# Key products as crossed 48x64 tiles, issued by turns with the corrected queries' products

## The chip, the cores and the metric

One core of one Trainium2 chip. The time is device microseconds (us) of one execution. A profile of one execution is taken apart from the timed runs. The engines go by short names: PE is TensorE (its matmuls; its weight loads stand apart as PEld), DVE is VectorE, ACT is ScalarE, POOL is GpSimd, SP is SyncE, which issues the loads.

## The reference

Three layers, one after the other: a delta-rule attention over 768 positions in 4 batches with 8 heads of 48, a mixing layer (Fourier transforms, then two products with a width of 1,536), and a gated layer with a product over positions. The change concerns the first:

```python
k_n = k / (np.linalg.norm(k, axis=-1, keepdims=True) + 1e-06)
state = np.zeros((B, H, D, D), dtype=np.float32)
for t in range(S):
    kt, vt, bt = (k_n[:, :, t], v[:, :, t], beta[:, :, t, None])
    y[:, :, t] = np.einsum('bhd,bhde->bhe', q[:, :, t], state)
    v_old = np.einsum('bhde,bhd->bhe', state, kt)
    state = state + bt[:, :, :, None] * np.einsum('bhd,bhe->bhde', kt, vt - v_old)
```

## The kernel before

**Tiling.** The positions are cut into chunks of 64; 4 batches of 12 chunks make 48 chunks, `bc`, in one order of their own (`SEQ`) in which the batches overlap. Heads go in four pairs, `hp`; of a pair one head lies on partitions 0 to 47 (or 63), the other on 64 to 111 (or 127). All products here are float32; one matmul of the program shows as two weight loads and two matmul records.

**Stages of a chunk.**
- `stage_a` (line 212): the key products. For each head pair, keys times queries and keys (64 rows by 128 columns) into the PSUM tile `pa` (bank X), which ACT copies out in two pieces (`copy_g`, lines 195 and 196) and, for later chunks, DVE masks (line 682).
- The triangular system made from them is solved on DVE in blocks of 8 chunks (`solve`, line 268): a generator, dealt out in shares to the steps (`part`, lines 615 and 616), so that DVE has solver work between the instructions that a step needs. `merge` and `diag` (lines 438 and 432) make the inverse of each chunk whole.
- `stage_b` (line 474): the inverse times keys and values, matmuls at line 480, copied out by ACT at line 482 (`WU`).
- `stage_c` (line 485): the products that correct the queries, 8 matmuls of 64 by 64 at line 495 into bank Y; DVE subtracts them at line 496 (`cw`).
- `stage_d` (line 499): state and output, 32 matmuls at lines 514 and 515.

**Forms of the key products.** Chunks 0 to 7 come first, by a path of their own (`pairs0`). Up to chunk 23 (`HEAD` is 24, line 31) `stage_a` does a pair of heads as two matmuls of 48 by 64, both on the diagonal of PE's array (`ROWS`, line 179; line 220): partitions 0 to 47 into output rows 0 to 63, partitions 64 to 111 into output rows 64 to 127. From chunk 24 on it does the pair as one matmul of 112 by 128 (line 222), for which the keys are laid out on the host as a block-diagonal matrix with zeros in the other blocks.

**Loads.** `load_kq` (line 202), on SP, in a pool of 5 buffers of 448 KB. For the head one load brings two chunks (`kc`: queries and keys only); from chunk 24 on one load brings one chunk (`kq`: queries, keys, and the block-diagonal keys twice as wide). The first five single loads stand in a table by step (`lead`, line 608); later ones are issued by `stage_a` of five chunks earlier. SP also issues the loads of the queries (`qt`), and of keys and values (`kv`), in program order.

**Steps.** The loop at line 609 runs `t` from -3 to 47. A step issues `stage_d(t)`, at times a `merge`, `stage_c(t + 1)`, a share of the solver, `stage_a` of a chunk 20 to 22 ahead (steps -3 to 1 for the rest of the head, steps 4 to 27 for chunks 24 to 47), `stage_b(t + 2)`, another `merge` at odd steps, and the rest of the solver's share. At the end of a step `self.chain()` fixes the order on each engine as written. Where `stage_c`'s chunk is the first of its batch, it has no products.

After the steps the mixing and gated layers follow (lines 693 to 1171).

Of the kernel before, what the change touches and what calls it, by code (L numbers as in the profile page):

```python
# [7 lines left out]
F32 = mybir.dt.float32  # L8
# [12 lines left out]
C = 64  # L21
# [45 lines left out]
class Kernel:  # L67
# [51 lines left out]
    def attention(self, cp, pg, pe, p, x, filler, after_solves):  # L119
# [59 lines left out]
        ROWS = (slice(0, D), slice(0, C)), (slice(64, 64 + D), slice(64, 64 + C))  # L179
# [22 lines left out]
        def load_kq(bc):  # L202
            if bc < HEAD:
                if 8 <= bc and bc % 2 == 0:
                    t = pe.tile([112, HP, 4 * C], F32, name="kq", bufs=CF["kq"]).rearrange("p a n -> p (a n)")
                    kqs[bc], kqs[bc + 1] = (t[:, i * HP * 2 * C : (i + 1) * HP * 2 * C].rearrange("p (a n) -> p a n", a=HP) for i in range(2))
                    load(out=t.rearrange("p (c n) -> p c n", c=2), in_=a["kc"][:, bc - 8 : bc - 6])
            elif bc < NBC:
                kqs[bc] = pe.tile([112, HP, 4 * C], F32, name="kq", bufs=CF["kq"])
                load(out=kqs[bc], in_=a["kq"][bc])  # L210

        def stage_a(bc):
            kq = kqs.pop(bc)
            if bc % 4 == 0:
                ring(bc)
            pa = self.bank("pa", [128, HP, 2 * C])
            for hp in range(HP):
                if bc < HEAD:
                    for r, q in ROWS:
                        nc.tensor.matmul(pa[q, hp], lhsT=kq[r, hp, C:], rhs=kq[r, hp], start=True, stop=True)  # L220
                else:
                    nc.tensor.matmul(pa[:, hp], lhsT=kq[:, hp, 2 * C :], rhs=kq[:, hp, : 2 * C], start=True, stop=True)
            if bc < HEAD:

                copy_g(gas[bc][:, :, C : 2 * C], pa[:, :, C:])
                nc.scalar.copy(out=gas[bc][:, :, :C], in_=pa[:, :, :C])
            else:
                copy_g(gas[bc][:, :, C : 2 * C], pa[:, :, C:])
                late.append((gas[bc][:, :, :C], pa[:, :, :C], mask_a(bc, C).to_broadcast([128, HP, C])))
            if bc < HEAD:  # L230
                if bc % 2 and bc + 2 * CF["kq"] < HEAD:
                    load_kq(bc + 2 * CF["kq"] - 1)
            else:
                load_kq(bc + CF["kq"])
            seen_a[0] = bc + 1
# [249 lines left out]
        def stage_c(bc):  # L485
# [6 lines left out]
            for hp in range(HP):  # L492
                for h in hs:

                    nc.tensor.matmul(pc[h, hp], lhsT=w[h, hp, :C], rhs=gas[bc][h, hp, : C + D], start=True, stop=True)  # L495
            nc.vector.tensor_sub(cw, qt, pc[:112])  # L496
# [111 lines left out]
        lead = {-2: (HEAD,), -1: (HEAD + 1,), 0: (HEAD + 2,), 1: (HEAD + 3,), 2: (HEAD + 4,)}  # L608
        for t in range(T0, NBC):
# [27 lines left out]
            if 0 <= t + 1 < NBC:  # L637
                stage_c(t + 1)
# [3 lines left out]
            if t + R + 2 < HEAD or HEAD <= t + R < NBC:  # L642
                stage_a(t + R + 2 * (t < 4))
            for bc in lead.get(t, ()):
                load_kq(bc)
# [690 lines left out]
def layout(q, k, v, beta, moe_w_ch1, moe_w_ch2, moe2_w_in, moe2_w_spatial, moe2_b_spatial, moe2_w_out):  # L1336
# [13 lines left out]
    kq = np.zeros((B, NC, 2, 64, HP, 4, C), f)  # L1350
    kq[:, :, :, :D, :, 0] = qt
    kq[:, :, :, :D, :, 1] = kt
    for h in range(2):
        kq[:, :, h, :D, :, 2 + h] = kt[:, :, h]
    kq = kq.reshape(NBC, 128, HP, 4 * C)[perm, :112]
    o["kq"] = kq

    o["kc"] = kq[8:HEAD, :, :, : 2 * C].transpose(1, 0, 2, 3).reshape(112, HEAD - 8, -1)
    o["kq0"] = np.stack([kq[:8, :, :, C : 2 * C], kq[:8, :, :, :C]]).transpose(0, 2, 1, 3, 4)
# [85 lines left out]
```

## Time and profile before

| what | us |
|---|---|
| timed runs, median | 853.3 |
| timed runs, lowest and highest | 852.4 and 856.03 |
| the profiled execution: span, first to last instruction | 849.6 |
| the profiled execution: its own time | not given beside the span |
| PE busy in the span | 806.9 |
| DVE busy | 606.6 |
| ACT busy | 419.8 |

The busy times of a page are sums over stages that differ. A stretch of the program is read from views that are cut to it: the busy time of each engine between two points of time, the timeline of an engine, and the list of who waited for whom. A wait that is marked "issue" is one for nothing that the profile shows. PEclk is the granted clock of PE as a share of full speed; the DMA share is the mean busy share of the 16 DMA engines.

### The profile page before, as it was taken

The page shows a single profiled execution, that of the slowest core. Times are in us where ns is not written, and L with a number is a line of the kernel's source. Part 1 is how long each engine was busy: PE and PEld are TensorE (multiplying, and loading weights), DVE is VectorE, ACT ScalarE, POOL GpSimd, SP SyncE. Part 2 cuts the span into 40 slices and gives each one's busy share as a digit, 9 for nine tenths or more (in the row PEclk, how much of TensorE's full clock was granted, in tenths as well). Part 3 has the DMA queues.
Part 4 walks back from the last instruction along what each step waited for, and adds up shares of the span by engine and source line. Part 5 has one row for each costly group of instructions (what it writes and reads, how often), then busy time and mean ns, then how long its engine had stood idle before and what let it go on. Part 6 is the DMA issues. An engine that isn't in the chain of part 4 may idle for free.

```text
span 849.6 us, 25166 instructions
## 1 busy us (share of the span) xinstructions
PE 806.9 (95%) x10507; PEld 769.6 (91%) x10507; DVE 606.6 (71%) x1791; ACT 419.8 (49%) x1070; POOL 6.3 (1%) x40
## 2 busy tenths in 40 slices
PE   7889999997888999999999999999999999999998
PEld 7778888876787999899999999999999899899998
DVE  7978898998969996692844992435678377586563
ACT  3669888887565544232233451223372462543632
POOL 1000000000000000000000000000000000000000
PEclk9779999999999999999999999999999999999999
DMA  8447666656532500001022410112001101101001
GB/s 241 109 124 181 187 170 191 166 162 177 148 106 60 204 1 1 1 1 29 1 72 80 131 34 22 38 57 66 29 3 47 64 12 46 57 23 59 32 1 56
DMA packets 57955, 67.63 MB, mean 80 GB/s; under 512 B 31857, under 2 KB 48978, under 8 KB 57842
## 3 DMA queue, kind: packets, MB, share of 16 engines
q1 hardware_dynamic: 57698, 65.89, 26.8%
q8 instruction: 82, 1.34, 0.7%
q14 instruction: 31, 0.25, 0.1%
q10 hardware_dynamic: 144, 0.15, 0.1%
HBM read 53.62 MB, written 4.72 MB: 69 GB/s over the span
## 4 chain that ended last, share of the span: by engine, by line
PE 67%; DVE 4%; issue 1%; ACT 1%; ACTq 0%
PE bankX L926 17%; PE bankY L939 15%; PE bankX L1124 10%; PE bankX L1104 6%; PE bankX L1072 6%; PE bankY L1152 5%; PE bankV L939 2%; PE bankX L739 2%; PE bankZ L1152 1%; PE bankX L755 1%; PE bankY L495 0%; PE bankX L733 0%; DVE cw L496 0%; DVE cvd L812 0%; PE bankY L515 0%
## 5 line engine op out<-in xcount | busy, mean ns | idle before, releaser
L939 PE MATMUL bankY<-w,hx 128*128 128x384 f32 x756 | 147.2, 336 | 0.0
L926 PE MATMUL bankX<-uh,w 128*128 128x384 f32 x504 | 137.7, 340 | 0.7 <-DVE ul L848 0.7
L939 PEld LDWEIGHTS bankY<-w,hx 128*128 128x128 f32 x756 | 132.4, 188 | 0.5 <-issue 0.3
L931 DVE SCALAR_TENSOR_TENSOR hx<-bankX,hx 128x384 fp32r<-128x384 f32 x84 | 46.2, 551 | 75.7 <-ACT hx L930 73.2
L930 ACT ACTIVATE hx<-bankX 128x384 fp32r<-128x384 f32 x84 | 41.2, 491 | 111.1 <-PE bankX L926 106.7
L926 PEld LDWEIGHTS bankX<-uh,w 128*128 128x128 f32 x504 | 92.1, 188 | 1.2 <-DVE ul L848 0.9
L1124 PE MATMUL bankX<-w,A 128*128 128x384 f32 x504 | 88.8, 334 | 0.0
L1124 PEld LDWEIGHTS bankX<-w,A 128*128 128x128 f32 x504 | 87.6, 188 | 0.0
L926 PE MATMUL bankX<-ul,w 128*128 128x384 f32 x252 | 85.1, 338 | 0.0
L495 PE MATMUL bankY<-gak,WU 64*64 64x112 f32 x704 | 45.3, 264 | 10.0 <-issue 6.2
L515 PE MATMUL bankY<-WU,gak 64*64 64x48 f32 x768 | 50.1, 224 | 1.1 <-ACT x L532 1.1
L1104 PE MATMUL bankX<-xh,s 128*128 128x384 f32 x192 | 50.0, 338 | 0.0
L314 DVE TENSOR_TENSOR Ts<-Ts,tm 128x108 f32<-128x108 f32 (+10 forms) x216 | 49.3, 265 | 0.9
L309 DVE TENSOR_TENSOR tm<-Ts 128x108 f32<-128x108 f32 (+10 forms) x216 | 48.9, 264 | 0.4
L1113 ACT CAST u<-hx 128x384 fp32r<-128x384 f32 x32 | 15.8, 513 | 66.0 <-DVE hx L1111 66.0
L514 PE MATMUL bankY<-WU,gak 64*64 64x48 f32 x704 | 43.8, 222 | 4.0 <-issue 4.0
L926 PEld LDWEIGHTS bankX<-ul,w 128*128 128x128 f32 x252 | 47.3, 188 | 0.0
L495 PEld LDWEIGHTS bankY<-gak,WU 64*64 64x64 f32 x704 | 35.6, 135 | 12.6 <-issue 7.1
L515 PE MATMUL bankY<-Sb,cw 48*64 48x48 f32 x704 | 46.0, 222 | 0.2
L514 PE MATMUL bankY<-Sb,cw 48*48 48x48 f32 x640 | 38.4, 208 | 8.2 <-DVE cw L496 4.9
L1072 PE MATMUL bankX<-s,xh 128*128 128x512 f32 x144 | 45.9, 395 | 0.0
L480 PE MATMUL bankY<-gak,TT 64*64 64x96 f32 x768 | 44.5, 256 | 1.2 <-ACT x L532 0.7
(237 smaller groups left out, 1827.7 us busy)
## 6 DMA issues: line engine op xcount, KB each, us to landing
kq<-in_kq_dram SPq DMA_DIRECT2D x24, 448.0 KB, 4.8
qt<-in_qt_dram SPq DMA_DIRECT2D x48, 196.0 KB, 4.1
gak<-in_kv_dram SPq DMA_DIRECT2D x48, 192.0 KB, 4.1
w<-in_w_dram SPq DMA_DIRECT2D x24, 384.0 KB, 6.9
out_dram<-x SPq DMA_DIRECT2D x24, 192.0 KB, 1.9
kq<-in_kc_dram SPq DMA_DIRECT2D x8, 448.0 KB, 9.8
x<-x SPq DMA_DIRECT2D x96, 36.0 KB, 1.9
s<-in_wi_dram SPq DMA_DIRECT2D x6, 512.0 KB, 4.3
```

The costliest lines, as they stand in the source:

```text
L309: nc.vector.tensor_tensor(out=tm, in0=T[:, r, k : k + 1].to_broadcast(sh), in1=T[:, k : k + 1, :k].to_broadcast(sh), op=MUL)
L314: nc.vector.tensor_add(o, o, tm)
L495: nc.tensor.matmul(pc[h, hp], lhsT=w[h, hp, :C], rhs=gas[bc][h, hp, : C + D], start=True, stop=True)
L514: nc.tensor.matmul(ps[C * i : C * i + n - C, hp], lhsT=k[:, C:n], rhs=u, start=not last, stop=end)
L515: nc.tensor.matmul(po[hs[1 - i], hp], lhsT=k[:, :C], rhs=u, start=not last, stop=end)
L926: nc.tensor.matmul(ph, lhsT=w1[f][i][:, c * 128 : c * 128 + 128], rhs=cur[k][:, c], start=(c + j == 0), stop=(c == 2 and j == 2))
L931: nc.vector.scalar_tensor_tensor(out=hl, in0=ph, scalar=0.0, in1=hh.bitcast(F32), op0=MAX, op1=SUB)
L939: nc.tensor.matmul(acc[t], lhsT=hx[i][:, t * 128 : t * 128 + 128], rhs=w2[e][k], start=(e == 0 and j == 0), stop=(e == 11 and j == 2),)
L1072: nc.tensor.matmul(pv, lhsT=xT[t][i][:, c, kk * 128 : kk * 128 + 128], rhs=wi[2 * c + 1][k], start=(c + j == 0), stop=(c == 2 and j == 2))
L1104: nc.tensor.matmul(pu, lhsT=wi[2 * c][i][:, f * 128 : f * 128 + 128], rhs=xT[hf][k][:, c], start=(c + j == 0), stop=(c == 2 and j == 2))
L1124: nc.tensor.matmul(acc, lhsT=A[:, m, o, i, kk], rhs=Bo[name, kk][:, k], start=(kk + j == 0), stop=(kk == 2 and j == 2))
L1152: nc.tensor.matmul(po, lhsT=a[:, :128], rhs=wo[f][k], start=(f + j == 0), stop=(f == last and j == 2))
```

## The change

Key products from chunk 24 on are computed as those of the head are, with two 48x64 matmuls for a head pair; the block-diagonal keys, their array in memory and their loads go. All chunks from 8 on are loaded two at a time from `kc`, in the same five buffers, each load issued by `stage_a` of the odd chunk nine ahead of it; the table `lead` goes. For all of them the tiles are crossed: the two heads' data change sides on the host (`::-1`), partitions 64 to 111 give output rows 0 to 63 and partitions 0 to 47 give output rows 64 to 127. `stage_c` becomes a generator that stops after each head pair; `stage_a` takes it and issues, for each head pair, its own two matmuls and then two of `stage_c`. For that `stage_a` stands where `stage_c` stood, ahead of the solver's share.

```diff
-        ROWS = (slice(0, D), slice(0, C)), (slice(64, 64 + D), slice(64, 64 + C))
+        ROWS = (slice(64, 64 + D), slice(0, C)), (slice(0, D), slice(64, 64 + C))
...
         def load_kq(bc):
-            if bc < HEAD:
-                if 8 <= bc and bc % 2 == 0:
-                    t = pe.tile([112, HP, 4 * C], F32, name="kq", bufs=CF["kq"]).rearrange("p a n -> p (a n)")
-                    kqs[bc], kqs[bc + 1] = (t[:, i * HP * 2 * C : (i + 1) * HP * 2 * C].rearrange("p (a n) -> p a n", a=HP) for i in range(2))
-                    load(out=t.rearrange("p (c n) -> p c n", c=2), in_=a["kc"][:, bc - 8 : bc - 6])
-            elif bc < NBC:
-                kqs[bc] = pe.tile([112, HP, 4 * C], F32, name="kq", bufs=CF["kq"])
-                load(out=kqs[bc], in_=a["kq"][bc])
-
-        def stage_a(bc):
+            if bc < NBC:
+                t = pe.tile([112, HP, 4 * C], F32, name="kq", bufs=CF["kq"]).rearrange("p a n -> p (a n)")
+                kqs[bc], kqs[bc + 1] = (t[:, i * HP * 2 * C : (i + 1) * HP * 2 * C].rearrange("p (a n) -> p a n", a=HP) for i in range(2))
+                load(out=t.rearrange("p (c n) -> p c n", c=2), in_=a["kc"][:, bc - 8 : bc - 6])
+
+        def stage_a(bc, other=iter(())):
...
             for hp in range(HP):
-                if bc < HEAD:
-                    for r, q in ROWS:
-                        nc.tensor.matmul(pa[q, hp], lhsT=kq[r, hp, C:], rhs=kq[r, hp], start=True, stop=True)
-                else:
-                    nc.tensor.matmul(pa[:, hp], lhsT=kq[:, hp, 2 * C :], rhs=kq[:, hp, : 2 * C], start=True, stop=True)
+                for r, q in ROWS:
+                    nc.tensor.matmul(pa[q, hp], lhsT=kq[r, hp, C:], rhs=kq[r, hp], start=True, stop=True)
+                next(other, None)
+            for _ in other:
+                pass
...
-            if bc < HEAD:
-                if bc % 2 and bc + 2 * CF["kq"] < HEAD:
-                    load_kq(bc + 2 * CF["kq"] - 1)
-            else:
-                load_kq(bc + CF["kq"])
+            if bc % 2:
+                load_kq(bc + 2 * CF["kq"] - 1)
...
                     nc.tensor.matmul(pc[h, hp], lhsT=w[h, hp, :C], rhs=gas[bc][h, hp, : C + D], start=True, stop=True)
+                yield
             nc.vector.tensor_sub(cw, qt, pc[:112])
...
-        lead = {-2: (HEAD,), -1: (HEAD + 1,), 0: (HEAD + 2,), 1: (HEAD + 3,), 2: (HEAD + 4,)}
...
-            if 0 <= t + 1 < NBC:
-                stage_c(t + 1)
+            corrected = stage_c(t + 1) if 0 <= t + 1 < NBC else iter(())
+            if t + R + 2 < HEAD or HEAD <= t + R < NBC:
+                stage_a(t + R + 2 * (t < 4), corrected)
+            for _ in corrected:
+                pass
             if light(t + 1) and t + 3 < NBC and (t + 3) % 8:
                 values(t + 3)
             part(c2)
-            if t + R + 2 < HEAD or HEAD <= t + R < NBC:
-                stage_a(t + R + 2 * (t < 4))
-            for bc in lead.get(t, ()):
-                load_kq(bc)
...
-    kq = np.zeros((B, NC, 2, 64, HP, 4, C), f)
-    kq[:, :, :, :D, :, 0] = qt
-    kq[:, :, :, :D, :, 1] = kt
-    for h in range(2):
-        kq[:, :, h, :D, :, 2 + h] = kt[:, :, h]
...
+    kq = np.zeros((B, NC, 2, 64, HP, 2, C), f)
+    kq[:, :, ::-1, :D, :, 0] = qt
+    kq[:, :, ::-1, :D, :, 1] = kt
```

On PE, a step of the stretch in which chunks 24 to 47 have their key products, between the end of `stage_d` and `stage_b`; `cw` marks the end of `stage_d`, `gak,WU` is `stage_c`, `kq` is `stage_a`, `gak,TT` is `stage_b`. Before:

```order
L514 MATMUL bankY<-Sb_93,cw 48x48
L515 MATMUL bankY<-Sb_93,cw 64x48
L495 MATMUL bankY<-gak,WU_92 64x112 x8
L222 MATMUL bankX<-kq 128x128 x4
L480 MATMUL bankY<-gak,TT_89 64x96 x8
```

The same step as changed, whose line numbers are those of the changed kernel:

```order
L510 MATMUL bankY<-Sb_93,cw 48x48
L511 MATMUL bankY<-Sb_93,cw 64x48
L217 MATMUL bankX<-kq 64x128 x2
L490 MATMUL bankY<-gak,WU_92 64x112 x2
L217 MATMUL bankX<-kq 64x128 x2
L490 MATMUL bankY<-gak,WU_92 64x112 x2
L217 MATMUL bankX<-kq 64x128 x2
L490 MATMUL bankY<-gak,WU_92 64x112 x2
L217 MATMUL bankX<-kq 64x128 x2
L490 MATMUL bankY<-gak,WU_92 64x112 x2
L475 MATMUL bankY<-gak,TT_89 64x96 x8
```

Four matmuls have become eight, and they stand among those of `stage_c`, two and two.

On SP, the loads from the head to about step 2; `kq<-in_kc_dram` is a load of two chunks, `kq<-in_kq_dram` one of a single chunk. Before:

```order
L105 DMA qt<-in_qt_dram 112x448 x2
L105 DMA kq<-in_kc_dram 112x1024 x3
L105 DMA gak<-in_kv_dram 128x4x96 x4
L105 DMA kq<-in_kq_dram 112x1024
L105 DMA qt<-in_qt_dram 112x448
L105 DMA kq<-in_kq_dram 112x1024
L105 DMA gak<-in_kv_dram 128x4x96 x2
L105 DMA qt<-in_qt_dram 112x448
L105 DMA kq<-in_kq_dram 112x1024
L105 DMA qt<-in_qt_dram 112x448
L105 DMA kq<-in_kq_dram 112x1024
L105 DMA gak<-in_kv_dram 128x4x96 x2
```

As changed:

```order
L105 DMA qt<-in_qt_dram 112x448 x2
L105 DMA kq<-in_kc_dram 112x1024 x5
L105 DMA gak<-in_kv_dram 128x4x96 x2
L105 DMA kq<-in_kc_dram 112x1024
L105 DMA gak<-in_kv_dram 128x4x96 x2
L105 DMA qt<-in_qt_dram 112x448
L105 DMA kq<-in_kc_dram 112x1024
L105 DMA gak<-in_kv_dram 128x4x96 x2
L105 DMA qt<-in_qt_dram 112x448 x2
L105 DMA kq<-in_kc_dram 112x1024
L105 DMA gak<-in_kv_dram 128x4x96 x2
```

Two loads more, for chunks 24 to 27, stand ahead of the first values; the single loads are gone, and pair loads stand further apart. The order on DVE is the same in both programs. On ACT, in two of the solver's blocks, a square root stands behind the two copies of `stage_a` instead of ahead of them.

## Rows read from the trace of the kernel before

**Rows 1.** The page, parts 1 and 3: busy us, instructions; the instruction queue's packets, MB.
```profile
PE 806.9 (95%) x10507; PEld 769.6 (91%) x10507; DVE 606.6 (71%) x1791; ACT 419.8 (49%) x1070; POOL 6.3 (1%) x40
...
q8 instruction: 82, 1.34, 0.7%
```

**Rows 2.** Stretches: us; PE, PEld, DVE, ACT, POOL busy (records); PEclk, DMA, GB/s.
```profile
72.00:182.00 110.00, 101.93 (x3054) 90.52 (x3048) 98.16 (x427) 96.00 (x304) 1.81 (x13) 1.00 0.64 180
182.00:240.00 58.00, 46.86 (x1701) 42.47 (x1698) 51.19 (x147) 38.36 (x104) 0.82 (x6) 0.97 0.57 160
272.00:320.00 48.00, 47.09 (x284) 46.06 (x279) 45.62 (x115) 25.20 (x61) 0.00 (x0) 1.00 0.30 108
```

**Rows 3.** PE's timeline in one step: start us, us, engine, line, operation, count.
```profile
109.74 0.27 PE L495 MATMUL bankY<-gak,WU 64*64 64x112 f32 x1
...
110.63 1.16 PE L222 MATMUL bankX<-kq 112*128 112x128 f32 x8
111.72 0.79 PE L480 MATMUL bankY<-gak,TT 64*64 64x96 f32 x13
```

**Rows 4.** PE's timeline in step 0; 31 records of 514/515 left out.
```profile
50.05 0.25 PE L514 MATMUL bankY<-WU,gak 64*64 64x48 f32 x1
...
50.55 0.97 PE L495 MATMUL bankY<-gak,WU 64*64 64x112 f32 x16
51.33 1.06 PE L220 MATMUL bankX<-kq 48*64 48x128 f32 x16
52.20 0.85 PE L480 MATMUL bankY<-gak,TT 64*64 64x96 f32 x16
```

**Rows 5.** Waits, 76 to 182 us: us in total, times, longest us.
```profile
DVE cw L496 <- PE bankY L495: 5.6, 8, 1.3
...
PE bankY L495 <- ACT WU L482: 3.6, 6, 0.8
```

**Rows 6.** DVE's timeline; in brackets the idle time before, and its releaser.
```profile
60.09 0.62 DVE L496 TENSOR_TENSOR cw<-qt,bankY 112x448 f32<-112x448 f32 x1 [3.31 <-PE bankY L495]
...
75.19 0.42 DVE L682 TENSOR_TENSOR gak<-bankX,mk 128x256 f32<-128x256 f32 x1 [3.18 <-ACT gak L196]
```

**Rows 7.** PE's timeline: five waits marked issue.
```profile
30.45 0.44 PE L404 MATMUL bankY<-Yh,V 32*32 32x16 f32 x31 [2.44 <-issue]
...
58.43 0.20 PE L514 MATMUL bankY<-WU,gak 64*64 64x48 f32 x1 [3.54 <-issue]
...
194.33 0.24 PE L514 MATMUL bankY<-Sb,cw 48*48 48x48 f32 x1 [1.52 <-issue]
...
199.51 0.44 PE L495 MATMUL bankY<-gak,WU 64*64 64x112 f32 x5 [1.05 <-issue]
...
202.97 0.20 PE L514 MATMUL bankY<-Sb,cw 48*48 48x48 f32 x1 [0.50 <-issue]
```

**Rows 8.** Busy time by stretch, as rows 2: two early stretches, two between stalls.
```profile
26.50:30.40 3.90, 1.52 (x161) 1.42 (x149) 3.83 (x6) 1.53 (x6) 0.68 (x5) 1.00 0.02 6
52.70:58.40 5.70, 2.20 (x134) 1.93 (x130) 4.08 (x23) 3.79 (x14) 0.00 (x0) 1.00 0.81 228
194.50:199.40 4.90, 3.96 (x126) 3.52 (x123) 3.59 (x13) 4.54 (x15) 0.00 (x0) 1.00 0.90 273
199.70:202.80 3.10, 2.77 (x127) 2.44 (x125) 2.61 (x7) 1.44 (x3) 0.00 (x0) 1.00 0.06 16
```

**Rows 9.** The page, part 6: single loads of kq: count, KB each, us.
```profile
kq<-in_kq_dram SPq DMA_DIRECT2D x24, 448.0 KB, 4.8
```

**Rows 10.** The load queue's timeline: single loads of kq (a fifth at 41.72).
```profile
39.51 0.61 SPq L105 DMA_DIRECT2D kq<-in_kq_dram  x1
...
51.83 0.42 SPq L105 DMA_DIRECT2D kq<-in_kq_dram  x1
...
52.76 0.42 SPq L105 DMA_DIRECT2D kq<-in_kq_dram  x1
...
65.66 0.42 SPq L105 DMA_DIRECT2D kq<-in_kq_dram  x1
```

More of the change, by code (lines that the diff above doesn't have):

```diff
@@ L1348, in layout @@
     kt = kr.transpose(0, 3, 2, 5, 1, 4)[..., KEY]
-    kq = np.zeros((B, NC, 2, 64, HP, 4, C), f)
-    kq[:, :, :, :D, :, 0] = qt
-    kq[:, :, :, :D, :, 1] = kt
-    for h in range(2):
-        kq[:, :, h, :D, :, 2 + h] = kt[:, :, h]
[L1355 to L1359, printed above, removed]
+    kq = np.zeros((B, NC, 2, 64, HP, 2, C), f)
+    kq[:, :, ::-1, :D, :, 0] = qt
+    kq[:, :, ::-1, :D, :, 1] = kt
+    kq = kq.reshape(NBC, 128, HP, 2 * C)[perm, :112]
+    o["kc"] = kq[8:].transpose(1, 0, 2, 3).reshape(112, NBC - 8, -1)
+    o["kq0"] = np.stack([kq[:8, :, :, C:], kq[:8, :, :, :C]]).transpose(0, 2, 1, 3, 4)
     qe = np.zeros((B, NC, 2, 64, HP, 112), f)
```

## The prediction

> **What bounds the kernel now.** I read the page's busy shares first, then the stretches of the program, then TensorE (PE) record by record where the change acts, then who waits for whom, and last PE's own idle time. Over the span PE is busy 95% [rows 1], which would make any PE work saved worth its full length. The stretches say otherwise. The change acts on the 24 steps between 72 and 182 us, and there all three engines are nearly full: of 110 us PE is busy 101.9, VectorE (DVE) 98.2, ScalarE (ACT) 96.0 [rows 2]. From 272 us on PE alone sets the pace (47.1 of 48 us) [rows 2], so whatever is won before that moves the end one for one.
>
> **A step on PE.** In a step the corrected queries (c, line 495) take from 109.74 to 110.63, 0.89 us, the key products (a, line 222) from there to 111.72, 1.09 us, then line 480 follows [rows 3]. At the end of the head, where a is already made of 48x64 tiles, c takes 0.78 us and a 0.87 us, one after the other [rows 4].
>
> **What the change does to that.** The key tiles now lie on the two quadrants of the array that c leaves free, and two records of each stand by turns.
> - Bounds for the merged group: with full overlap the longer part, 0.87 us; with none the sum, 0.78 + 0.87 = 1.65 us [rows 4].
> - The nearest row for four busy quadrants is line 514/515, which uses all four: from 50.05 to 50.55 stand 32 records of it, one per 15.6 ns, with 48 columns each. c, on two quadrants, starts 16 records of 112 columns in 0.78 us, 48.8 ns each, which scales to 20.9 ns for 48 columns [rows 4]. 15.6 is under 20.9, so more than two quadrants do work at once. I take 0.95 us, near the lower bound.
> - PE work saved: 0.89 + 1.09 - 0.95 = 1.03 us a step, 24 steps, 24.7 us; with the upper bound 0.33 us a step, 7.9 us.
>
> **Why most of it does not arrive, first reason: DVE.** Between 72 and 182 us DVE is idle 110.0 - 98.2 = 11.8 us [rows 2]. 3.18 us of that is one wait for ACT at 75.19 us, in the first step of the stretch [rows 6]. What PE can give back is the waits for c, 5.6 us in 8 [rows 5]; with the shorter ones for the copies of a, which the list breaks up, I call it 6 us. DVE's order is the same in both programs, and its work is not cut, so about 6 us is the ceiling of this stretch.
>
> **Second reason: PE's own instructions.** The queue called "instruction" brought 82 packets, and PE executed 10,507 matmuls and as many weight loads [rows 1]: 256 to a packet. PE's waits marked "issue", for nothing that the profile shows, stand one such packet apart: between the stalls ending at 194.33 and 199.51 us there are 126 + 123 records, between 199.51 and 202.97 us 127 + 125 [rows 7, 8]. So PE runs dry until the next 256 instructions are there. From stall to stall the first took 5.18 us while the DMA engines were 0.90 busy, the second 3.46 us while they were 0.06 busy [rows 7, 8]. A straight line through the two gives 4.66 us at the 0.64 share of the stretch 72 to 182. In that stretch PE executes 3,054 + 3,048 records [rows 2], 23.8 packets, and 23.8 x 4.66 = 111 us: that is the 110 us it takes. The stretch already runs at about the pace at which instructions arrive, and PE's execution merely fits under it.
>
> The Trainium skill (Runtime: NRT & Kernel Launch, "Instruction fetch mechanics") says that instructions come in blocks of 16 KiB, 256 of them, and that crossing a block's end is mostly hidden. This trace agrees on the block and not on the hiding: PE stood 3.54 us at one such place and 2.44 us at another [rows 7]. By that rule the second reason falls away and the DVE ceiling alone would hold, which is the first rival below.
>
> **The change in packets.** Each step gets four matmuls more, each with two weight loads and two passes: 16 records, 384 over 24 steps, so 6,486 records or 25.3 packets. Against that, 24 loads of 448 KB become 12 of the same size [rows 9]. Five of the 24 are issued between 39.51 and 65.66 us [rows 10], ahead of the stretch, and five of the 12 will be (two in the head, three by step 1), so in the stretch 19 become 7: 12 x 0.459 MB = 5.5 MB of 180 GB/s x 110 us = 19.8 MB go. The DMA share falls from 0.64 to about 0.46, and the line gives 4.29 us a packet: 25.3 x 4.29 = 108.7 us, 2.3 under the line's 111 and 1.3 under the measured 110. **I take -2 us.** The bounds are 25.3 x 3.46 = 87.5 us, where DVE's ceiling of -6 us cuts in, and 25.3 x 5.18 = 131 us; the pace must stay under 110 / 25.3 = 4.35 us for any gain.
>
> **Before the stretch.** The loads of chunks 24 to 27 move. Now two of them are issued at 51.83 and 52.76 us [rows 10], just ahead of the 3.54 us stall that ends at 58.43; DVE waits 3.31 us on the products behind it [rows 6, 7]. Between 52.7 and 58.4 us the DMA share is 0.81 at 228 GB/s, 1.30 MB [rows 8]. These two loads are 0.92 MB of it. Without them the share would be some 0.24, and the line gives 3.8 instead of 5.2 us: -1.4. They are replaced by pair loads in the head, which must wait only for chunks 15 and 17 and so land on 24 to 30 us. From 26.5 to 30.4 us the DMA engines are 0.02 busy now, and PE still stalls 2.44 us there [rows 7, 8]; a full queue makes that packet 5.2 us instead of 3.4: up to +1.8, of which I take +1.3, since the loads begin before the packet is asked for. Step 0 has a head chunk beside c: 0.78 + 0.87 - 0.95 = -0.7. Step 1 has one too, behind the stalled place: nothing. Sum **-0.8 us**, bounds -4 and +1.8.
>
> **What costs nothing.** A pair load waits on the load queue for the products of its second chunk, with the next queries' and values' loads behind it, as each single load does for its chunk now; there are half as many of these waits. One square root on ACT moves behind two copies, in two blocks of the solver; DVE's 11.8 idle us cover it, and without this cover it would cost those two copies twice. A wait of c for ACT now holds up the later key tiles too, but they stood behind c before. After 182 us nothing is changed; 384 more records (1.5 packets) shift where the "issue" stalls fall among 182 to 240 us, where PE is idle 11 of 58 us [rows 2]: 0, with 2 us either way.
>
> **Sum.** -2 - 0.8 = -2.8 us against the profiled execution, whose span is 849.6 us. No time of its own is given beside the span; the median of the runs, 853.3 us, is 3.7 us over it, and I keep that distance. 853.3 - 2.8 = 850.5 us.
>
> **The rivals.**
> 1. *DVE sets the pace.* PE waits more often for DVE and ACT, and while it stands at such a wait the next packet can arrive unseen. Then the stretch gains the 6 us that DVE has to give, and with the 0.8 before it the time is 846.5 us. For: c's matmuls wait for ACT 3.6 us in 6 even now [rows 5], and a faster PE meets more such waits. Against: it also reaches the end of each packet earlier. The rule of the Trainium skill that is cited above would make this the likeliest case. Chance 0.25.
> 2. *Slower: the packets' pace is not relieved.* If the DMA share does not set it and 110 / 23.8 = 4.62 us a packet stays, 25.3 packets take 116.9 us, +6.9; the head's +1.3 stays and the -1.4 does not come: with -0.7 it is +7.5, 861 us. It decides from 4.35 us a packet on. For: 1.5 packets more are certain, and the line rests on two points. Against: both packets with a full queue are the slow ones. Chance 0.15.
> 3. *The quadrants do not overlap* (two streams through the same rows exclude each other), so that the change does not do what it says: 0.33 us a step of PE work is left, and the packets' pace holds the rest. About 853 us. Against: 15.6 ns a record in line 514/515. Chance 0.08.
>
> **How the numbers follow.** The forecast has 0.48, the rivals 0.25, 0.15 and 0.08, and 0.04 is left for mishaps of either sign. A measurement of this kernel can tell about 0.5%, 4.3 us, from no change. The forecast's own range, from the bounds before and after the stretch, is 846 to 854 us, and a third of its chance (0.16) is more than 4.3 us faster. Faster: 0.25 + 0.16 + 0.01 = 0.42. Same: 0.32 + 0.08 + 0.02 = 0.42. Slower: 0.15 + 0.01 = 0.16. The range 842 to 858 holds the forecast and the first and third rival whole, and the lower part of the second.
>
> **What would show it.** Right: from the first record of the merged group to the first of `stage_b` about 1.0 us; PE's busy time from 72 us on falls by over 20 us while the stretch shrinks by 1 to 4; more and longer "issue" waits on PE; fewer waits of DVE for c. The first rival shows in a stretch shorter by 5 us or more and few "issue" stalls; the second in a stretch longer than 112 us with stalls at nearly each packet; the third in a group of 1.6 us. The forecast is wrong if the 3.54 us stall is still there, if the head grows by over 2 us, or if PE's clock, 1.00 throughout the stretch now [rows 2], falls because PE stands more.

## The result and the profile after

The changed kernel took 844.34 us, median of 4 runs (841.91 to 846.83), beside 854.66 us for the kernel before (4 runs): ratio 0.9885, 95% interval 0.9846 to 0.9924. Two later measurements, beside the experiments, gave 0.9919 (0.9889 to 0.9949) and 0.9913 (0.9881 to 0.9946), 850.9 against 856.5 us and 850.6 against 857.3. It is faster, by 0.8 to 1.2%: 7 to 10 us by the ratios, 5.6 to 10.3 by the medians, where 2.8 were forecast. A ratio here is not the quotient of the two medians, which differs from it by up to 0.0016.

The page after, parts 1, 3 and 6 [against rows 1 and 9]:

```profile
PE 788.9 (94%) x10699; PEld 752.2 (90%) x10699; DVE 605.0 (72%) x1791; ACT 419.6 (50%) x1070; POOL 6.3 (1%) x40
...
q1 hardware_dynamic: 56162, 60.38, 24.9%
q8 instruction: 84, 1.38, 0.7%
...
kq<-in_kc_dram SPq DMA_DIRECT2D x20, 448.0 KB, 4.4
```

PE lost 18 us of busy time, yet executes 192 matmuls and as many weight loads more, and two packets of instructions more were brought.

The stretch after [against rows 2]; columns are the stretch, its length, busy us (records) of PE, PEld, DVE, ACT and POOL, then PEclk, DMA share and GB/s:

```profile
72.00:182.00 110.00, 89.34 (x3366) 78.61 (x3360) 102.85 (x434) 96.89 (x309) 2.47 (x18) 0.97 0.49 133
```

In the same 110 us PE is busy 12.6 us less and DVE 4.7 us more: DVE gets through its work faster, PE stands more. The DMA share fell from 0.64 to 0.49.

To compare equal work, the stretches below are cut at events: the end of the fourth `cw` of VectorE's line `tensor_sub(cw, ...)`, of the 25th, and of the last (44 are in each trace). The first piece, which holds the 24 steps with key products, is called **the steps**, the second **what follows**. Kernel before (columns as above):

```profile
71.40:181.32 109.92, 101.85 (x3074) 90.55 (x3071) 98.09 (x427) 96.05 (x303) 1.81 (x13) 1.00 0.65 181
181.32:270.91 89.59, 74.05 (x2422) 67.08 (x2422) 75.94 (x210) 56.85 (x153) 0.82 (x6) 0.98 0.43 121
```

Changed kernel, first trace:

```profile
70.20:175.85 105.65, 86.94 (x3275) 76.62 (x3276) 97.37 (x427) 94.07 (x301) 1.80 (x13) 0.97 0.49 134
175.85:261.59 85.74, 72.43 (x2402) 65.85 (x2403) 75.60 (x209) 56.78 (x153) 0.83 (x6) 0.98 0.45 127
```

The same kernel in the two later measurements, one fence for each:

```profile
72.61:179.66 107.05, 86.50 (x3274) 76.40 (x3276) 97.31 (x428) 94.23 (x301) 1.81 (x13) 0.97 0.50 132
179.66:268.34 88.68, 72.53 (x2402) 66.10 (x2403) 76.01 (x210) 56.70 (x153) 0.83 (x6) 0.98 0.43 123
```

```profile
72.92:181.45 108.53, 89.40 (x3274) 79.26 (x3276) 97.36 (x428) 94.40 (x301) 1.80 (x13) 0.94 0.49 131
181.45:270.53 89.08, 73.27 (x2402) 66.55 (x2403) 76.04 (x209) 56.84 (x153) 0.82 (x6) 0.98 0.44 122
```

In the steps PE was idle 109.92 - 101.85 = 8.1 us before; in the three traces after it is 18.7, 20.6 and 19.1 us. DVE's busy time is the same within 0.8 us, so the steps are shorter by what DVE is idle less: 11.8 us before, 8.3, 9.7 and 11.2 after. Behind the last `cw` the span is 578.5 to 578.7 us in all four traces: what is won or lost lies ahead of it.

**Packet ends.** PE's instructions come in packets of 256. Counted through a trace in order of their start (weight loads, matmuls and the few that only wait), the places where PE stands for "issue" lie 256 apart. Of PE's idle time in the steps 3.5 us stand at these places before, and 12.6, 14.0 and 13.1 us in the three traces after; the idle time elsewhere is 4.5 us before and 6.1, 6.6 and 6.0 after. So the new idle time is mostly at packet ends.

**The merged group**, PE's timeline of the changed kernel (start us, us, engine, line, operation, count) [against rows 3]:

```profile
83.55 0.31 PE L490 MATMUL bankY<-gak,WU 64*64 64x112 f32 x1
...
83.64 0.30 PE L217 MATMUL bankX<-kq 48*64 48x128 f32 x2
...
84.37 0.25 PE L475 MATMUL bankY<-gak,TT 64*64 64x96 f32 x2
```

From the first record to the first of `stage_b` it is 0.82 us, where it was 109.74 to 111.72, 1.98 us. This is the group at its shortest: of the 21 in the steps of this trace that have both kinds of products, seven take 0.82 to 0.85 us and the others 1.0 to 2.5, median 1.24. In the kernel before 18 of 20 take 1.97 to 2.06.

**Who waits**, between 76 and 182 us: total, times, longest [against rows 5]:

```profile
PE bankY L510 <- issue: 5.1, 5, 1.6
...
DVE cw L492 <- PE bankX L217: 2.6, 4, 1.0
...
DVE cw L492 <- PE bankY L490: 2.3, 2, 1.6
```

DVE's waits for c, 5.6 us in 8 before, are 2.3 in 2, and 2.6 in 4 are new: there the profile names the crossed tiles as what came last.

**The two early stalls**, PE's timeline [against rows 7], the idle time in brackets:

```profile
31.91 0.44 PE L399 MATMUL bankY<-Yh,V 32*32 32x16 f32 x31 [2.44 <-issue]
...
57.55 0.20 PE L510 MATMUL bankY<-WU,gak 64*64 64x48 f32 x1 [1.34 <-issue]
```

The head's stall ends 1.46 us later than before; the one of 3.54 us is down to 1.34.

### The profile page after: what moved, and what is told of

Its sections match the earlier page's. It is cut to its first block, busy times and chain, and to the rows that moved or that the text cites. A ratio compares the mean times of both kernels' runs of the same rounds, so it can differ in the third digit from the quotient of the medians.

```text
span 840.1 us, 25514 instructions
## 1 busy us (share of the span) xinstructions
PE 788.9 (94%) x10699; PEld 752.2 (90%) x10699; DVE 605.0 (72%) x1791; ACT 419.6 (50%) x1070; POOL 6.3 (1%) x40
## 4 chain that ended last, share of the span: by engine, by line
PE 68%; DVE 4%; ACT 1%; issue 1%; ACTq 0%
PE bankX L920 17%; PE bankY L933 15%; PE bankX L1118 10%; PE bankX L1098 6%; PE bankX L1066 6%; PE bankY L1146 5%; PE bankV L933 2%; PE bankX L733 2%; PE bankZ L1146 1%; PE bankX L749 1%; PE bankY L511 0%; PE bankY L490 0%; DVE cw L492 0%; PE bankX L727 0%; PE bankY L475 0%
## 5 line engine op out<-in xcount | busy, mean ns | idle before, releaser
L511 PE MATMUL bankY<-WU,gak 64*64 64x48 f32 x768 | 52.2, 226 | 5.1 <-issue 2.9
L510 PE MATMUL bankY<-WU,gak 64*64 64x48 f32 x704 | 47.5, 224 | 6.5 <-issue 6.5
L217 PE MATMUL bankX<-kq 48*64 48x128 f32 x640 | 49.3, 296 | 2.3 <-issue 2.3
L511 PEld LDWEIGHTS bankY<-WU,gak 64*64 64x64 f32 x768 | 40.6, 136 | 9.5 <-issue 4.5
L475 PEld LDWEIGHTS bankY<-gak,TT 64*64 64x64 f32 x768 | 38.6, 140 | 10.7 <-ACT gak L467 2.4
```

What stands on the lines that cost most here:

```text
L475: nc.tensor.matmul(pb[h, hp].rearrange("p t d -> p (t d)"), lhsT=tt[h, o + hp], rhs=kv[h, hp], start=True, stop=True)
L510: nc.tensor.matmul(ps[C * i : C * i + n - C, hp], lhsT=k[:, C:n], rhs=u, start=not last, stop=end)
L511: nc.tensor.matmul(po[hs[1 - i], hp], lhsT=k[:, :C], rhs=u, start=not last, stop=end)
```

## The experiments

Two theories were tried. **A**: what PE saves is taken by its instructions: it stands at the ends of packets of 256, and more records, or more load on the DMA engines, make it stand longer. **B**: DVE sets the pace, and stalls only fill time that PE has left. All times are medians; "beside" is the kernel before in the same measurement.

| run | us | beside | ratio, interval | steps us | PE idle there | at packet ends | PEclk |
|---|---|---|---|---|---|---|---|
| changed, again (first) | 850.9 | 856.5 | 0.9919, 0.9889 to 0.9949 | 107.05 | 20.6 | 14.0 | 0.97 |
| single loads | 853.7 | 856.5 | 0.9957, 0.9929 to 0.9985 | 112.32 | 22.8 | 18.4 | 0.92 |
| no turns | 851.4 | 856.5 | 0.9944, 0.9911 to 0.9976 | 110.32 | 20.5 | 14.0 | 0.97 |
| same quadrants | 853.4 | 856.5 | 0.9952, 0.9919 to 0.9985 | 110.65 | 11.8 | 7.0 | 0.98 |
| pair loads alone | 855.6 | 857.0 | 0.9985, 0.9960 to 1.0010 | 109.86 | 7.5 | 3.6 | 1.00 |
| more instructions | 857.2 | 857.0 | 1.0007, 0.9984 to 1.0030 | 112.64 | 21.6 | 19.7 | 0.95 |
| no key loads | 848.1 | 857.0 | 0.9892, 0.9853 to 0.9930 | 107.00 | 18.4 | 11.7 | 0.95 |
| more DVE | 857.8 | 857.0 | 1.0009, 0.9987 to 1.0031 | 113.13 | 20.1 | 9.8 | 0.91 |
| changed, again (second) | 850.6 | 857.3 | 0.9913, 0.9881 to 0.9946 | 108.53 | 19.1 | 13.1 | 0.94 |
| more loads | 873.4 | 857.3 | 1.0186, 1.0156 to 1.0216 | 130.44 | 28.7 | 24.2 | 0.82 |
| fewer records, ACT | 859.7 | 857.3 | 1.0027, 1.0000 to 1.0054 | 109.93 | 6.4 | 0.3 | 0.94 |
| fewer records, DVE | 873.1 | 857.3 | 1.0165, 1.0122 to 1.0207 | 123.05 | 4.9 | 0.3 | 0.83 |

Against the changed kernel's 0.9916 (mean of its two ratios here) 0.0010 is 0.86 us; two ratios are told apart from about 0.004, 3.5 us, on. The last four columns are of one trace each; the same program gave steps of 105.65 to 108.53 us in three.

**The changed kernel again.** No edit.

> The changed kernel once more, unaltered, so that the three experiments stand beside it on one chip. Expected: 844 us, within 0.4% (841 to 847), the steps from 72 to 182 us of the kernel before 5 us shorter than there.

> The changed kernel once more, beside the next three. Expected: a ratio to the kernel before between 0.987 and 0.993, in the ranges of its two measurements so far (0.9885 and 0.9919).

The second ratio fell into the expected range. The first run's time did not, 850.9 us instead of 841 to 847, with the kernel before 2 us slower as well; its steps were 2.9 us shorter than before instead of 5.

**Single loads.** Crossed tiles and turns kept, loads as before:

```diff
-            if bc < NBC:
+            if bc >= HEAD:
+                if bc < NBC:
+                    kqs[bc] = pe.tile([112, HP, 4 * C], F32, name="kq", bufs=CF["kq"])
+                    load(out=kqs[bc], in_=a["kq"][bc])
+            elif bc % 2 == 0:
...
```

> The crossed tiles and the turns stay; the key loads go back to one load of 448 KB for each chunk from the 24th on, issued where the kernel before issues them. Theory A (the instruction packets set the pace of the steps and fewer bytes relieve it, as in the prediction): the share of the DMA engines in the steps rises from 0.49 back to about 0.62, the packets come in 4.6 us again instead of 4.1, and 25 packets cost 25 x 0.5 = 12 us more, less the 1.4 us that the head wins: about 855 us, slower than the kernel before by up to 2. Theory B (the gain of the steps comes from the products, and DVE sets the pace): the steps keep their 5 us; the head wins 1.5 us and the stall ahead of the steps, 1.4 us in the changed kernel, is 3.5 us again: 844 to 846 us.

```profile
72.32:184.64 112.32, 89.55 (x3275) 80.50 (x3277) 97.58 (x427) 94.88 (x302) 1.82 (x13) 0.92 0.65 176
```

The loads' share is back at 0.65. The ratio is 0.0041 above the changed kernel's, 3.5 us, just at what can be told apart, and lies between B's 0 to 2 and A's 11. PE's idle time at packet ends is 18.4 us instead of 12.6 to 14.0. The packets come every 4.36 us (112.32 x 256 / 6,591 instructions of PE) instead of 4.10, 4.16 and 4.22; A had expected 4.6.

**No turns.** c whole, then a, on the same quadrants as in the changed kernel:

```diff
             corrected = stage_c(t + 1) if 0 <= t + 1 < NBC else iter(())
+            for _ in corrected:
+                pass
```

> The pair loads and the crossed tiles stay; the corrected queries' products are issued whole and then the key products, as many instructions as in the changed kernel. The two groups should take 0.78 + 0.87 = 1.65 us instead of 0.82, 20 us more of PE's work in 24 steps. Theory A (packets set the pace, and PE's execution fits under it): PE is 89 us busy of 105 in the steps now, so 16 of the 20 us fit into its idle time: 844 to 850 us, with shorter packet stalls. Theory B (PE's execution counts, through what DVE waits for): DVE waits for each group 0.8 us longer where it waits at all, 8 steps or more, and the gain of the steps is gone: 850 to 856 us.

Some 2.4 us longer than the changed kernel, within A's 0 to 6, but the premise was wrong. PE's timeline of one step:

```profile
88.15 0.27 PE L490 MATMUL bankY<-gak,WU 64*64 64x112 f32 x1
...
88.62 0.33 PE L217 MATMUL bankX<-kq 48*64 48x128 f32 x2
88.65 0.35 PE L490 MATMUL bankY<-gak,WU 64*64 64x112 f32 x3
...
89.12 0.30 PE L475 MATMUL bankY<-gak,TT 64*64 64x96 f32 x2
```

Issued one after the other, the two still overlap: key products start at 88.62 while c's records are still starting, and `stage_b` starts at 89.12 before the last key tile. Where nothing interrupts them it is 0.92 to 0.97 us from the first record to `stage_b`, not 1.65, though the last key tile starts only 1.24 to 1.29 us after the first record (0.82 to 0.92 in the changed kernel). For `stage_b` the turns are worth some 0.1 us a step; in the time they are not told apart from nothing.

**The same quadrants.** Turns kept, tiles back on the diagonal:

```diff
-        ROWS = (slice(64, 64 + D), slice(0, C)), (slice(0, D), slice(64, 64 + C))
+        ROWS = (slice(0, D), slice(0, C)), (slice(64, 64 + D), slice(64, 64 + C))
...
```

> Loads and turns stay; the key tiles go back to the two quadrants on the diagonal, the same that the corrected queries use, so that the records of the two still stand by turns but no longer on four quadrants. If the quadrants are what overlaps, the merged group takes 1.6 to 1.75 us instead of 0.82, and the time is that of the kernel without turns within 2 us. If taking turns is what counts (loads of one behind passes of the other), the group stays under 1.1 us and the time at 844 us.

```profile
88.98 0.28 PE L217 MATMUL bankX<-kq 48*64 48x128 f32 x1
...
90.65 0.39 PE L475 MATMUL bankY<-gak,TT 64*64 64x96 f32 x4
```

1.67 us, as expected of the first case: it is the free quadrants that overlap, not the turns. And this is the best measure of what PE's execution is worth here: 0.85 us more in each of 24 steps, 20 us, with not one record more, cost some 3 us by the ratios, which is not clear of nothing. The window shows where they went:

```profile
74.78:185.43 110.65, 98.89 (x3275) 91.08 (x3277) 97.72 (x428) 96.22 (x304) 1.81 (x13) 0.98 0.47 129
```

PE is busy 9.5 to 12.4 us longer than in the changed kernel and idle 11.8 us instead of 19 to 21, at packet ends 7.0 instead of 12.6 to 14.0. The time that the crossed tiles free is time in which PE then waits.

**Pair loads alone.** The kernel before with the changed kernel's loads; GpSimd writes the diagonal blocks:

```diff
-                    nc.tensor.matmul(pa[:, hp], lhsT=kq[:, hp, 2 * C :], rhs=kq[:, hp, : 2 * C], start=True, stop=True)
+                    nc.tensor.matmul(pa[:, hp], lhsT=BD[bc % 3][:, hp], rhs=kq[:, hp], start=True, stop=True)
...
+                for r, q in ROWS:
+                    nc.gpsimd.tensor_copy(out=BD[n % 3][r, :, q], in_=kqs[n][r, :, C:])
...
```

> The other half of the change alone: the kernel before with the changed kernel's loads (one of 448 KB for two chunks). The block-diagonal keys, which these loads no longer bring, are laid out by GpSimd, two copies a chunk, two chunks ahead; the corrected queries and the key products are as in the kernel before, whole and one after the other, with 16 records for the key products instead of 32. Theory A (the packets of instructions set the pace of the steps, and their pace follows the load on the DMA engines): 24.2 packets at 4.2 us instead of 4.55 would be 8 us less, but PE is 102 us busy of 110 and DVE's waits leave it about 4: 850 to 853 us. Theory B (the gain comes from the shorter products): 855 to 858 us, as before.

```profile
74.22:184.08 109.86, 102.38 (x3062) 90.67 (x3063) 101.51 (x428) 95.67 (x302) 35.88 (x55) 1.00 0.49 130
```

With the share at 0.49 instead of 0.65 the steps take 109.86 us, as before, and PE is idle 7.5 us against 8.1, at packet ends 3.6 against 3.5. The kernel before was not paced by its packets. One thing clouds it: DVE's busy time is 3.4 us longer beside GpSimd's copies (GpSimd is busy 35.88 us), which could hide a gain of that size; PE's idle time says there was little to gain.

**More instructions.** Four matmuls of one column a step, written over by the real ones:

```diff
+            for r, q in ROWS * 2 if bc >= HEAD else ():
+                nc.tensor.matmul(pa[q, 0, :1], lhsT=kq[r, 0, C:], rhs=kq[r, 0, :1], start=True, stop=True)
```

> The changed kernel with four more key products of a single column in each of the 24 steps, written over by the real ones: 16 records a step, 384 in all, 1.5 packets, and at 15.6 ns a record 6 us of PE's time at most, where PE stands idle for some 20 us. Theory A (packets set the pace): 1.5 x 4.1 = 6 us longer, 850 us where the changed kernel has 844, or 857 where it has 851. Theory B (DVE sets the pace, packets only fill PE's idle time): 0 to 2 us longer.

```profile
71.92:184.56 112.64, 91.05 (x3462) 82.50 (x3462) 97.85 (x428) 95.16 (x301) 1.81 (x13) 0.95 0.48 126
```

The whole gain is gone: 1.0007 - 0.9916 is 7.8 us. Where nothing interrupts it, the merged group grew by 0.13 to 0.19 us only (0.82 to 0.95 and 1.01), 4.6 us in 24 steps at most, while 20 us of pure execution cost some 3. The packets came every 112.64 x 256 / 6,965 = 4.14 us, as in the changed kernel, only 1.5 more of them, and PE's idle time at packet ends rose from 12.6 to 14.0 us to 19.7, while the idle time elsewhere fell from some 6 to 1.9. This is A. Part of the contrast goes with the clock: its mean over the runs is 0.969 here, 0.978 on the same quadrants and 0.974 in the changed kernel, by the estimate in the next section (0.55 us for 0.001) some 3 us more here and 2 us less there.

**No key loads** from chunk 28 on.

```diff
+            if HEAD + 4 <= bc < NBC:
+                kqs[bc], kqs[bc + 1] = kept
...
```

> The changed kernel without the loads of queries and keys for chunks 28 to 47: they take those of chunks 26 and 27 again, so the output is not the reference's. Ten loads of 448 KB go, seven of them out of the steps, 3.2 MB of the 14.6 MB there. Theory A (the packets' pace follows the DMA load): the share falls from 0.49 to about 0.38 and 25.7 packets come in about 3.95 instead of 4.13 us: 4 to 5 us less than the changed kernel. Theory B (DVE sets the pace): within 1.5 us of the changed kernel.

Some 2 us less than the changed kernel (0.9892 against 0.9916), where A had 4 to 5; it is not told apart from nothing, and the steps, at a share of 0.39, are no shorter (107.00 us). Inconclusive: below the share of the changed kernel little is to be had.

**More DVE.** The mask twice:

```diff
                 nc.vector.tensor_tensor(out=out, in0=m0, in1=m1, op=MUL)
+                nc.vector.tensor_tensor(out=out, in0=m0, in1=m1, op=MUL)
```

> The changed kernel with the mask of the key products multiplied twice by DVE, in 24 steps: 24 x 0.42 = 10 us more of DVE's work, which is idle for 8 to 10 us of the steps. Theory B (DVE sets the pace): 8 to 10 us longer than the changed kernel. Theory A (packets set the pace and DVE follows): 0 to 5 us longer, as DVE's idle time takes it up.

```profile
71.68:184.81 113.13, 93.00 (x3274) 82.45 (x3276) 106.56 (x450) 94.89 (x301) 1.80 (x13) 0.91 0.47 126
```

8 us longer, as B expected; in its trace 2.3 us of it lie behind the last `cw`, beside a granted clock of 0.98 to 0.99 where it was 1.00. DVE has 106.56 us to do instead of 97.4 and its idle time only falls from 8.3-11.2 to 6.6 us. PE's idle time stays at 20.1 us, but only 9.8 of it at packet ends: a part of it has moved to waits for DVE. So A and B are both true of the changed kernel: PE's stalls and DVE's work follow one another in a loop (c, `cw`, the next step's products) with little slack, and either engine's delay is passed on.

**More loads.** Two loads that nobody reads beside each of seven key loads:

```diff
+                for i in range(2 if bc >= HEAD + 10 else 0):
+                    load(out=JK[i].rearrange("p (c n) -> p c n", c=2), in_=a["kc"][:, bc - 8 : bc - 6])
...
```

> The changed kernel with two loads of 448 KB more beside each of the seven key loads that are issued in the steps (from chunk 34 on); what they bring is read by nobody. That is 6.4 MB more in the steps, as much as the pair loads saved and a little more. Over the ten traces so far the packets that PE had to wait for take 3.64 us with the 16 DMA engines idle and 0.069 us more for each engine that is busy. Theory A: the share rises by some 0.22, 3.5 engines, 0.24 us a packet, 25.7 packets: 6 us longer than the changed kernel, or 4 if part of it falls where PE has other waits. Theory B (the DMA load does not matter): within 1.5 us of the changed kernel.

23 us longer, four times what A expected. The stretch and three pieces of it:

```profile
73.44:203.88 130.44, 101.75 (x3274) 91.58 (x3276) 97.89 (x428) 95.18 (x301) 1.80 (x13) 0.82 0.63 158
...
84.90:89.25 4.35, 0.01 (x1) 0.00 (x1) 2.81 (x16) 1.72 (x6) 0.00 (x0) 0.71 0.96 200
86.76:93.59 6.83, 4.34 (x110) 4.12 (x111) 2.34 (x12) 1.92 (x6) 0.00 (x0) 0.50 0.39 84
...
97.03:101.22 4.19, 0.01 (x1) 0.00 (x0) 0.00 (x0) 2.77 (x9) 0.00 (x0) 0.90 0.89 208
```

The end of a packet that falls into a burst of three loads makes PE stand 4.35 and 4.19 us, not some tenths longer: by the records of the instruction queue such a packet begins to move 4.4 to 5.0 us after the one before it was used up, where those between the bursts mostly need 1.0 to 1.3. So what counts is what stands ahead in that moment, not the mean share. And during the first of these stalls the granted clock fell to 0.50, 1.2 GHz, until 93.59. 47.8 of the 130.4 us ran at that level; in the changed kernel 6.8, 6.8 and 13.7 us.

**Fewer records.** One product for each head gives output and state; ACT, or ACT and DVE, copy the state in two pieces (the copies are left out here):

```diff
-                        if ps is not None:
-                            nc.tensor.matmul(ps[C * i : C * i + n - C, hp], lhsT=k[:, C:n], rhs=u, start=not last, stop=end)
-                        nc.tensor.matmul(po[hs[1 - i], hp], lhsT=k[:, :C], rhs=u, start=not last, stop=end)
+                        n = n if c < NC - 1 else C
+                        nc.tensor.matmul(pd[i][:n, hp], lhsT=k[:, :n], rhs=u, start=not last, stop=end)
...
```

> The changed kernel with half the records in the stage of outputs and states: for each head one product of 112 or 128 columns instead of one of 64 columns for the output and one of 48 or 64 for the state, so 64 records a step instead of 128. The state of the two heads then lies in two banks and ScalarE copies it in two pieces, 0.31 us more in each step. Theory A (packets set the pace of the steps and of most of what follows up to 260 us): 6 packets fewer in the steps and 5 after them; at 4.1 us they are worth 45 us, of which DVE and ACT, idle for some 9 us in the steps, leave 5 to 8 there, less what ACT's extra 7 us take, and some 5 us after: 6 to 10 us less than the changed kernel. Theory B (DVE or ACT sets the pace): ACT has 7 us more to do: 0 to 5 us longer.

> The same, with the second piece of the state copied by DVE instead of ScalarE, where it stands behind nothing but waits for the products of its own step. Theory A: 6 to 10 us less than the changed kernel, as with ScalarE, and which of the two is better tells which of the two engines is next: if ScalarE's 97 us in the steps are the next bound this one is faster by 2 us or more. Theory B: 0 to 5 us longer than the changed kernel.

```profile
72.53:182.46 109.93, 103.53 (x2596) 95.32 (x2598) 97.56 (x428) 100.28 (x324) 1.81 (x13) 0.94 0.49 129
```

Both are slower than the changed kernel, by 10 and 21 us, and A's expectation was wrong, in an instructive way: the stalls did go (PE idle 6.4 us instead of 19 to 21, of which 0.3 at packet ends), but PE is busy 103.5 us. The group that was halved runs longer:

```profile
108.14 0.42 PE L508 MATMUL bankY<-WU,gak 64*128 64x48 f32 x4
...
109.66 0.36 PE L508 MATMUL bankY<-Sb,cw 48*112 48x48 f32 x4
```

32 records take from 108.14 to about 109.8, 1.6 us; the 64 on four quadrants take 0.93 us wherever nothing interrupts them, before and after the change alike. PE's execution is again the fullest, as in the kernel before, whose PE was busy 101.85 us; ACT's 100.28 us, 6 more than in the changed kernel, were not separated from it. With the second copy on DVE it is worse; the steps, and DVE's waits at that copy (total, times, longest):

```profile
72.32:195.37 123.05, 118.11 (x2618) 108.62 (x2618) 106.80 (x450) 96.44 (x306) 1.80 (x13) 0.83 0.43 115
...
DVE Sb L517 <- PE bankY L508: 5.0, 3, 2.9
```

DVE has 9 us more to do and stands 5.0 us in 3 waits at that copy, and the granted clock is 0.83: 41.1 us of the steps ran at 1.2 GHz. What each of them takes of the 21 us stays open. None of these runs with the reference's result is faster than the changed kernel.

## Why the prediction was right, and where not

**The merged group: right where nothing interrupts it.** 0.95 us was taken, 0.82 measured at its shortest; with packet ends, waits and the lower clock the median is 1.24. The reason given, more than two quadrants at work, is shown by the run on the same quadrants (1.67 us). That the turns do it was not claimed, and they hardly do.

**PE's busy time: too much.** "Falls by over 20 us" was to be seen; 12.6 us in the fixed window, 12.5 to 15.4 between the events. A part of the difference is the half clock, in which PE is busy longer with the same work: 6.8 to 13.7 us of the steps ran at it, by estimate up to half of that, 3.4 to 6.9 us. The rest was not traced.

**DVE's ceiling: right.** DVE's idle time fell by 0.7 to 3.6 us of the 6 allowed, and doubling the mask shows DVE close to the loop's length. Its waits for c did shrink, but the crossed tiles are now among what `cw` waits for (2.6 us).

**The packets: right for the changed kernel, wrong for the kernel before.** The step that failed is "The stretch already runs at about the pace at which instructions arrive, and PE's execution merely fits under it." Two things were wrong in it.
- The line through two stalls was twice too steep. Over ten traces (both kernels' first ones and the first eight of the table) 212 packets between 70 and 240 us made PE stand over 0.4 us at their end; a line through them gives 3.64 us a packet with the DMA engines idle and 0.069 us for each busy one of 16, 1.1 us over the whole range, and the packets scatter by some 0.5 us about it. The prediction had 2.05. By this line 23.8 packets at a share of 0.64 take 103.5 us, not the 111 that seemed to equal the measured 110: the agreement was a coincidence.
- Fewer loads alone changed nothing (pair loads alone). The kernel before was paced by PE's execution and its loop with DVE; at packet ends in the steps PE was idle 3.5 us before, and 12.6, 14.0 and 13.1 us after.

So the expected gain was taken by packets, but in the other order: the shorter groups moved the bound from PE's execution to its instructions, at 25.75 packets in 4.10 to 4.22 us. 4.29 had been forecast for it, with a share of 0.46 (measured 0.49), and the point from which no gain is left, 4.35, is nearly what the single loads show (4.36, and steps of 112 us). The result for the steps, -2, is near the three traces' -4.3, -2.9 and -1.4, and that is in part luck: it was the difference of two sums on a line that was too steep, of which only the second was the pace of its kernel.

The Trainium skill (Runtime: NRT & Kernel Launch, "Instruction fetch mechanics") has the crossing of a block mostly hidden. The trace of the changed kernel disagrees: PE was idle 12.6 of 105.65 us at the ends of packets, and the run with four small matmuls more a step, 7.8 us longer, shows that this is paid for.

**Before the steps: the parts right, their sum not told.** The 3.54 us stall fell to 1.34 (1.4 had been forecast to go, 2.2 went; by the prediction's own line a share of 0.81 gives 5.0 us and not 5.2, so 1.2); the head's stall ends 1.46 us later (1.3 forecast). The steps begin at 70.20, 72.61 and 72.92 us in the three traces, at 71.40 before: -1.2, +1.2 and +1.5, where -0.8 was forecast. The granted clock bears on this: ahead of the steps 20.5, 34.1 and 34.1 us ran at 1.2 GHz in the three, 23.9 before, so executions of one program differ here by more than the forecast.

**After the steps: 0, with 2 us either way.** What follows took 3.8, 0.9 and 0.5 us less. The first trace has few stalls there, 3.4 us of idle time at packet ends; the same program had 9.1 and 9.0 in the next two, and the kernel before 9.1, so this is no effect of the shifted packets.

**The time.** 850.5 us were forecast and 844.34 measured: under the forecast's own 846 to 854, inside the outer 842 to 858. The sum of -2.8 us against the trace before compares with -9.5, -2.8 and -0.6 us of the three spans, -4.3 in the mean. The runs say -7 to -10. The term that failed here is "the median of the runs, 853.3 us, is 3.7 us over it, and I keep that distance": in the runs of the changed kernel the time is 1.8 us over the span of the same run (841.91 to 840.1), so the trace of the kernel before was of an execution of about 851.4 us, some 5 us under the medians of 856.5 to 857.3 that 76 later runs of it gave. With 1.8 the same sum gives 848.6 us. A part of the 5 us is the clock: in that trace 27.3 of 849.6 us ran at 1.2 GHz, a mean of 0.984 where those 76 runs have 0.979, and among them 0.001 goes with 0.36 us, so some 2 us by this estimate. With only one trace of it, where its usual runs spend the rest stays open, and so does how much of the gain each stage has in them.

**The signs.** More and longer waits for "issue": yes. The forecast was to be wrong if PE's clock falls because PE stands more, and it does fall: 0.97, 0.97 and 0.94 in the steps, 1.00 before. It takes some of the gain. In the second repeat the granted clock fell to 0.50 at 102.36 us, while PE stood 2.00 us for "issue". The stretch, and PE's timeline in it:

```profile
102.36:105.77 3.41, 2.98 (x60) 2.98 (x61) 1.30 (x8) 1.72 (x7) 0.00 (x0) 0.50 0.33 74
```

```profile
102.79 0.23 PE L510 MATMUL bankY<-Sb,cw 48*48 48x48 f32 x1 [2.00 <-issue]
102.80 0.47 PE L217 MATMUL bankX<-kq 48*64 48x128 f32 x1
...
104.36 0.38 PE L475 MATMUL bankY<-gak,TT 64*64 64x96 f32 x2
```

There the merged group took 1.56 us instead of 0.82. Over the span the mean clock of the changed kernel's 19 runs is 0.974, of the kernel before's 76 runs 0.979; among those 19 runs 0.001 goes with 0.55 us, so by that estimate the lower clock costs some 3 us. That idle time alone brings the clock down is not shown: with fewer records and the copy on DVE PE was idle 4.9 us of the steps, not once for over 0.2 us up to 92.92 us, and the clock was 0.50 from the start of the steps to there.

**The rivals.** The first (DVE sets the pace, 846.5 us) is nearest in size, but its sign, few "issue" stalls, is missing. The second needed more than 4.35 us a packet; the run with more loads shows that world (5.07 us, slower by 1.9%). The third is the case that the run on the same quadrants sets up; its gain was priced too low: that run still has a ratio of 0.9952, where 853 against 853.3 us was said.

## What to carry to other kernels

Work taken off an engine that is fully busy is worth only the distance to the next bound, and that bound can be the engine's own instruction stream: count records as well as columns, and doubt a split that doubles them once PE begins to stand at packet ends. The opposite trade (half the records, each over twice the columns of the array) can be worse still; look at busy and idle together. A rate read from two stalls is not a law, and a sum that agrees with the measured length is no proof that the stretch runs at that rate: the check is to change one factor alone. And one profiled execution has its own luck: compare its time with the medians before sums are made against it.

## What was not expected of the hardware

- Two groups of products on different quadrants overlap even when one is issued wholly after the other: from the first record to the next stage 0.92 to 0.97 us, against 0.82 by turns and 1.67 on the same quadrants (to the start of the last key tile 1.24 to 1.29, 0.82 to 0.92 and 1.59 to 1.68).
- A burst of loads delays the next packet of instructions: stalls of 4.2 to 4.4 us beside three loads of 448 KB, with the granted clock at 0.50 from inside one of them on. 6.4 MB that nobody reads cost 23 us, with 8 to 10 us more of PE's idle time and 34 to 41 us more of the steps at 1.2 GHz.
- DVE's work in the steps took 101.5 us beside 34 us of GpSimd's copies, and 97.3 to 98.1 without them, for the same 427 to 428 instructions.
